# Attention and feed-forward on one core: the context halves and output turns of a step put in a new order, the last turn held into the next step, the output transposes halved

## Chip, cores, metric

One core of a Trainium2 chip. The metric is the device time of one execution in microseconds (us); lower is better. Ratios between kernels are the mean time of one kernel's fast runs over the mean of the other's fast runs of the same rounds, so they are not quite the ratio of the medians quoted beside them.

## The reference, cut to what matters

```python
xn = layernorm(x)                                   # x: 2048 x 640
# 32 heads of 192; keys and values are the last 512 rows of the caches
q = xn @ wq
p = softmax(q_h @ k_h.T * 192**-0.5)                # per head
s = concat_h(p @ v_h) @ wo                          # 6144 -> 640
g = silu((silu(xn @ w_gate) * (xn @ w_up)) @ w_down)
out = x + s * g
```

## The kernel before

After the feed-forward part (some 168 us) the kernel works through 16 pairs of heads (`pr`), and in each pair through 4 blocks of 512 query rows (`b`); a step is `i = 4 * pr + b`. A pair has two stages. First come the scores of its four steps, woven with the q blocks of the steps after. Then come the four context and output stages. A step's output uses the transposed context of two steps earlier.

Every matmul of these stages contracts 64 rows and runs beside a partner on the other half of the array ("row tiles"); only in the context and output stages of the last two pairs is the full array used. The two partners write different banks of PSUM, the matmul's accumulator memory. In contexts and outputs they change banks after the first "turn", so a second turn may start only when the first has ended. That is enforced by a tiny GpSimd memset which waits for the first turn and for which the second turn waits. Other PE work stands between the turns to hide it.

There are two kinds of PSUM accumulators with two buffers each: "sc" (scores, output tiles) and "mm" (q blocks, contexts).

```python
psum = ctx.enter_context(tc.tile_pool(name="psum", bufs=2, space=bass.MemoryType.PSUM))
def sc_tile(): return psum.tile([P, 2, 512], f32, name="sc", tag="sc")
def mm_tile(): return psum.tile([P, 2, 512], f32, name="mm", tag="mm")
...
def pv(i, q2):                      # contexts of half q2: four parts of 8 matmuls; 0,1 are turn 0, 2,3 turn 1
    ...                             # part 0: acc = mm_tile() (sc_tile() in one early case)
    #   after part 1: turned(m, st)    after part 3: divide(i, q2, acc, ...)
def divide(i, q2, acc, alone):      # VectorE reciprocal, four ScalarE scalings into O_b (bufs=2)
    ...
    if pr == last or i == 0:        # transpose by halves
        nc.sync.dma_start_transpose(out=OT_b[:, 6*q2 : 6*q2+6, :], in_=O_b[:, 2*q2 : 2*q2+2, :, :]...)
    elif pr < last and q2 == 1:     # both halves at once, after the second
        nc.sync.dma_start_transpose(out=OT_b[:, :, :], in_=O_b[:, :, :, :]...)
...
def turned(m, st):                  # the first turn's last matmul -> a memset on GpSimd
    st["turn"] = nc.gpsimd.memset(turn_t[:], 0.0)
    follows(st["turn"], m)          # `after` makes the second turn follow the memset
def wo_tile(i, qt):                 # one output tile: two turns of six matmuls
    def first():
        st["sc"] = sc_tile()
        wo_turn(st, i, qt, 0)
    def second():
        wo_turn(st, i, qt, 1)
        ...                         # VectorE: s_t = s_t + sc
    return [first, second]
...
def woven(x, y, z):                 # x: a context half, y and z: two output tiles
    for part in (y[0], *x[:2], y[1], z[0], *x[2:], z[1]):
        part()
...
for pr in range(NPAIR):
    for b in range(NB):
        i = pr * NB + b
        for kc in range(KC):
            if kc < 3 and i + 1 < NS:
                q_rows(i + 1, kc)   # ten matmuls into mm_tile(), then a VectorE sum into qT
            scores(i, kc)           # six matmuls into sc_tile(), then a ScalarE Exp
            ...
    for b in range(NB):
        i = pr * NB + b
        if i < 2:
            two(pv(i, 0), pv(i, 1))
        else:
            for q2 in range(2):
                if pr < last - 1:
                    woven(pv(i, q2), wo_tile(i - 2, 2 * q2), wo_tile(i - 2, 2 * q2 + 1))
                else:
                    ...             # the last two pairs: full-array matmuls, no turns
        ...                         # loads for later pairs, on the same sync queue as the transposes
```

The softmax here doesn't subtract the row's maximum and nothing guards it: scores larger than these inputs give would overflow.

## Time and profile before

| | before |
|---|---|
| time, median of the runs at hand | 938.76 us (938.25 to 939.03) |
| profiled span | 936.9 us |
| PE busy | 98% of it |
| one undisturbed pair of heads | 47.67 us |

The pair is read from the table of engines by stretches of time. Its columns are the stretch and its length, then busy time (and instructions) of each engine, the granted clock, the share of DMA and the rate moved.

```profile
core 0: us, PE busy (x) PEld busy (x) DVE busy (x) ACT busy (x) POOL busy (x), PEclk, DMA share, GB/s
234.55:282.22 47.67, 47.21 (x664) 33.90 (x664) 32.76 (x46) 26.80 (x49) 2.36 (x24) 1.00 0.42 80
```

PE is idle for only 0.46 us of this pair by its rows. In the page's list of DMA issues the transposes of the context stand like this (the last number is the median from issue to landing):

```profile
OT_b<-O_b SPq DMA_TRANSPOSE x67, 3.8
```

In this document DVE is VectorE, ACT is ScalarE, POOL is GpSimd and SPq is the sync engine's queue. Line 428 is the q block, 442 the scores, 446 the Exp, 468 the contexts. Line 568 (563 where the code is five lines shorter) is the output turn.

### The profile page before, as it was taken

Reading aid. Unit: us, or ns where it says so; the run is one execution under the profiler, and the core shown is the slowest. Engines: PE = TensorE matmul, PEld = TensorE weight load, DVE = VectorE, ACT = ScalarE, POOL = GpSimd, SP = SyncE. Lnnn points to the kernel's source line nnn. Section 1 sums busy time; section 2 is a strip of 40 time slices with the busy share of each in tenths; the row PEclk is TensorE's granted clock in tenths of the full one; section 3 lists DMA queues with packets and bytes.
Section 4 is the critical chain, followed back from the end, with each engine's and each line's share of the span. In section 5 each row is a group of like instructions: output and inputs, shape, how many; then the busy total and the mean of one; then the engine's idle time right before and its main releaser. Section 6 shows DMA issues by size and latency. Waiting matters only on the chain.

```text
span 936.9 us, 25618 instructions
## 1 busy us (share of the span) xinstructions
PE 920.3 (98%) x11101; PEld 613.0 (65%) x11101; DVE 576.7 (62%) x844; ACT 474.5 (51%) x847; POOL 100.2 (11%) x387
## 2 busy tenths in 40 slices
PE   9999999999999999999999999999999999999998
PEld 5455556474858575858686767576767767666665
DVE  6433321567676767676667666676767676767655
ACT  4222223646464646464646565555555555556561
POOL 0000000000100000000000000000000000002977
PEclk9999999999999999999999999999999999999999
DMA  9321510053534334443435253527161716163524
GB/s 296 69 60 27 113 34 1 1 101 63 92 71 88 75 73 90 72 92 66 97 59 105 55 109 50 113 35 129 36 127 32 129 25 135 25 128 91 133 57 138
DMA packets 241921, 77.17 MB, mean 82 GB/s; under 512 B 222736, under 2 KB 241808, under 8 KB 241808
## 3 DMA queue, kind: packets, MB, share of 16 engines
q1 hardware_dynamic: 240752, 74.71, 38.5%
q8 instruction: 87, 1.43, 0.6%
q10 hardware_dynamic: 1056, 0.82, 0.3%
q14 instruction: 26, 0.21, 0.1%
HBM read 39.45 MB, written 2.62 MB: 45 GB/s over the span
## 4 chain that ended last, share of the span: by engine, by line
PE 94%; DMA 3%; ACT 2%; DVE 1%; issue 0%; SPq 0%; DVEq 0%
PE mm L428 22%; PE sc L568 18%; PE sc L442 17%; PE mm L468 14%; PE sc L276 11%; PE mm L298 6%; PE sc L542 3%; DMA OT_b<-O_b 3%; PE mm L525 2%; ACT p_t L446 1%; PE sc L219 1%; PE mm L276 0%; PE mm L311 0%; PE sc L525 0%; ACT O_b L498 0%
## 5 line engine op out<-in xcount | busy, mean ns | idle before, releaser
L446 ACT ACTIVATE p_t<-sc 128x1024 bf16<-128x1024 f32 x254 | 253.1, 1023 | 117.5 <-PE sc L442 117.4
L433 DVE TENSOR_REDUCE qT<-mm 128x512 bf16<-128x1024 f32 x189 | 231.3, 1224 | 102.5 <-PE mm L428 100.0
L498 ACT ACTIVATE O_b<-mm,r 128x192 bf16<-128x192 f32 x486 | 165.1, 422 | 207.6 <-issue 107.1
L428 PE MATMUL mm<-xnT,wq_p 64*128 64x512 bf16 x1890 | 236.8, 376 | 0.0
L568 PE MATMUL sc<-wo_p,OT_b 64*128 64x320 bf16 x2592 | 217.5, 296 | 10.6 <-ACT p_t L446 6.0
L593 DVE TENSOR_TENSOR sacc<-sacc,sc 128x640 f32<-128x640 f32 x200 | 164.2, 821 | 89.7 <-PE sc L568 89.7
L442 PE MATMUL sc<-qT,khat 64*128 64x512 bf16 x1524 | 197.4, 376 | 0.0
L468 PE MATMUL mm<-V_p,p_t 64*128 64x193 bf16 x3520 | 185.7, 242 | 0.0
L468 PEld LDWEIGHTS <-p_t 64*128 64x128 bf16 x3584 | 161.4, 93 | 11.2
L428 PEld LDWEIGHTS <-wq_p 64*128 64x128 bf16 x1890 | 101.4, 94 | 100.4 <-issue 0.8
L568 PEld LDWEIGHTS <-OT_b 64*128 64x128 bf16 x2592 | 135.9, 94 | 39.0 <-issue 9.9
L442 PEld LDWEIGHTS <-khat 64*128 64x128 bf16 x1536 | 82.4, 94 | 83.3
L556 POOL MEMSET turn_t<- 128x1 f32 x328 | 32.2, 98 | 709.4 <-PE sc L568 544.4
L284 DVE TENSOR_TENSOR hT<-sc,sg 128x512 bf16<-128x512 f32 x46 | 31.7, 690 | 85.2 <-ACT sg L283 85.1
L283 ACT ACTIVATE sg<-sc 128x512 bf16<-128x512 f32 x46 | 27.3, 596 | 72.4 <-PE sc L276 72.4
L276 PE MATMUL sc<-xnT,wg_sb 128*128 128x512 bf16 (+1 forms) x260 | 59.2, 354 | 0.0
L276 PE MATMUL sc<-xnT,wu_sb 128*128 128x512 bf16 (+1 forms) x260 | 59.1, 354 | 0.0
L298 PE MATMUL mm<-wd_sb,hT 128*128 128x320 bf16 x384 | 56.6, 299 | 0.0
L487 DVE RECIPROCAL r<-mm 128x4 f32<-128x4 f32 x124 | 22.7, 183 | 48.9 <-PE mm L468 35.7
L298 PEld LDWEIGHTS <-hT 128*128 128x128 bf16 x384 | 37.6, 98 | 18.9
L276 PEld LDWEIGHTS <-wu_sb 128*128 128x128 bf16 x285 | 26.4, 98 | 26.9
L276 PEld LDWEIGHTS <-wg_sb 128*128 128x128 bf16 x285 | 26.4, 98 | 23.1 <-DMA wg_sb<-in_B_w_gate_dram 0.2
(67 smaller groups left out, 373.3 us busy)
## 6 DMA issues: line engine op xcount, KB each, us to landing
wo_p<-in_A_wo_dram SPq DMA_DIRECT2D x16, 480.0 KB, 4.3
K_p<-in_A_k_cache_dram SPq DMA_DIRECT2D x32, 192.0 KB, 3.8
V_p<-in_A_v_cache_dram SPq DMA_DIRECT2D x32, 192.0 KB, 3.1
wq_p<-in_A_wq_dram SPq DMA_DIRECT2D x64, 80.0 KB, 3.4
wq_p<-in_A_wq_dram SPq DMA_DIRECT2D x16, 160.0 KB, 3.5
x_r<-in_A_x_dram SPq DMA_DIRECT2D x16, 160.0 KB, 4.0
x_t<-in_A_x_dram SPq DMA_DIRECT2D x14, 160.0 KB, 3.6
wd_sb<-in_B_w_down_dram SPq DMA_DIRECT2D x1, 1920.0 KB, 12.4
```

The lines of the kernel that those rows point to most:

```text
L276: nc.tensor.matmul(out, w_sb[:, c, f * P : (f + 1) * P], xnT[:, c, qc], start=(c == 0), stop=(c == NC - 1),)
L284: nc.vector.tensor_tensor(hTs[b][:, f, :], u, sg[:], ALU.mult)
L298: nc.tensor.matmul(dn[:, 0:HD], hTs[b][:, f, ti * P : (ti + 1) * P], wd_sb[:, f, cols], start=(f == 0), stop=(f == NF - 1),)
L428: nc.tensor.matmul(q_ps[:, h, :], pairs[pr]["wq"][r, c, j * P : (j + 1) * P], xnT[r, c, b * 512 : (b + 1) * 512], start=(c == 0), stop=(c ...
L433: nc.vector.reduce_sum(qTs[i][:, j, :], q_ps[:, :, :].rearrange("p h n -> p n h"), axis=AX.X)
L442: nc.tensor.matmul(sc[:, h, :], khat[r, j, ks], qT[r, j, :], start=(j == 0), stop=(j == 2))
L446: nc.scalar.activation(p_t[:, :, :], sc[:, :, :], ACT.Exp, scale=scale)
L468: m = nc.tensor.matmul(acc[:, k, h * 256 : h * 256 + Dh + 1], Ps[i][kc][r, h, qt * P : (qt + 1) * P], V_p[r, kc, h, 0 : Dh + 1], start=(p ...
L498: nc.scalar.activation(O_b[:, qt, h, :], a_k[:, h, 0:Dh], ACT.Copy, scale=r[:, k, h, :])
L556: st["turn"] = nc.gpsimd.memset(turn_t[:], 0.0)
L568: m = nc.tensor.matmul(ps[:, n, 0:HD], OTs[i][r, 3 * qt + j, :], pairs[i // NB]["wo"][r, j, n * HD : (n + 1) * HD], start=(turn == 0 and j ...
L593: nc.vector.tensor_tensor(s_t, s_t, sc[:, :, 0:HD], ALU.add)
```

## The change

The intent: contexts first, so that PE has work at a pair's start while both "sc" buffers still hold scores; one step as a unit of two context halves and four output tiles, with more room between a half and its transpose's use; transposes by halves, so that each starts as soon as its half is done. The step's last turn has no work left to hide its memset, so it is held into the next step.

```diff
@@ divide
-        if pr == last or i == 0:
-            nc.sync.dma_start_transpose(
-                out=OT_b[:, 6 * q2 : 6 * q2 + 6, :],
-                in_=O_b[:, 2 * q2 : 2 * q2 + 2, :, :].rearrange("p t h d -> p (t h d)"),
-            )
-        elif pr < last and q2 == 1:
-            nc.sync.dma_start_transpose(
-                out=OT_b[:, :, :], in_=O_b[:, :, :, :].rearrange("p t h d -> p (t h d)")
-            )
+        nc.sync.dma_start_transpose(
+            out=OT_b[:, 6 * q2 : 6 * q2 + 6, :],
+            in_=O_b[:, 2 * q2 : 2 * q2 + 2, :, :].rearrange("p t h d -> p (t h d)"),
+        )
@@
-    def woven(x, y, z):
-        for part in (y[0], *x[:2], y[1], z[0], *x[2:], z[1]):
+    def drop():
+        while held:
+            held.pop()()
+
+    def woven(i):
+        (a, b), (w, x, y, z) = (pv(i, 0), pv(i, 1)), (wo_tile(i - 2, qt) for qt in range(4))
+        for part in (*a[:2], drop, w[0], *b[:2], w[1], x[0], *a[2:], x[1], y[0], *b[2:], y[1], z[0]):
             part()
+        held.append(z[1])
@@ the main loop
                     q_rows(i + 1, kc)
+                    drop()
                 scores(i, kc)
...
+            elif pr < last - 1:
+                woven(i)
```

More of the change, by code (lines that the diff above doesn't have):

```diff
@@ L652, in store @@
             nc.sync.dma_start(out=out2[t * P : (t + 1) * P, :], in_=ob[:])
+    held = []
     def two(x, y):
@@ L690 @@
                 two(pv(i, 0), pv(i, 1))
+            elif pr < last - 1:
+                woven(i)
             else:
                 for q2 in range(2):
-                    if pr < last - 1:
-                        woven(pv(i, q2), wo_tile(i - 2, 2 * q2), wo_tile(i - 2, 2 * q2 + 1))
-                    else:
-                        pv_full(i, q2)
-                        wo_full(i - 2, 2 * q2)
-                        wo_full(i - 2, 2 * q2 + 1)
+                    pv_full(i, q2)
+                    wo_full(i - 2, 2 * q2)
+                    wo_full(i - 2, 2 * q2 + 1)
             if b == 0 and pr + 2 < NPAIR:
```

## The prediction

> **What bounds the kernel now.** I read the busy table first, then the chain of work that ended last, then who waited for whom on the TensorE (PE), then the order of time around each kind of wait.
>
> ```profile
> PE 920.3 (98%) x11101; PEld 613.0 (65%) x11101; DVE 576.7 (62%) x844; ACT 474.5 (51%) x847; POOL 100.2 (11%) x387
> ...
> PE 94%; DMA 3%; ACT 2%; DVE 1%; issue 0%; SPq 0%; DVEq 0%
> ```
>
> PE is busy 98% of a 936.9 us span and 94% of the chain is PE work; the change leaves the number and shapes of its matmuls as they are. So it can only win time in which PE stands still. A matmul's row lasts longer than its turn (the chain gives six of the 320-column ones 0.41 us although one row lasts 0.296), so part of each stall hides under the last row. I therefore measure stalls from start to start: next start minus the last start's regular pace. By this measure the blocks run at a pace set by columns alone: ten q matmuls take 1.08 us, six score matmuls 0.65, sixteen context matmuls (two "parts") 0.67, six output matmuls (one "turn") 0.405. A change between kinds costs about 0.01 us, so changes of order are nearly free. What stands out are two kinds of stall:
>
> ```profile
> PE sc L568 <- ACT p_t L446: 6.0, 13, 0.5
> PE sc L568 <- DMA OT_b<-O_b: 3.6, 5, 1.2
> PE sc L568 <- DVE sacc L593: 0.9, 1, 0.9
> ```
>
> Line 568 is the output turn. Thirteen times, once for each head pair from the second to the fourteenth, it waits for an Exp (line 446); six times for a transpose by DMA (the one put down to DVE is at 342.79 us, where a transpose issued at 337.30 landed 5.45 later). First kind, in order of time:
>
> ```profile
> 424.33 1.48 PE L442 MATMUL sc<-qT,khat 64*128 64x512 bf16 x12
> 424.55 1.22 DVE L433 TENSOR_REDUCE qT<-mm 128x512 bf16<-128x1024 f32 x1
> 425.20 1.94 ACT L446 ACTIVATE p_t<-sc 128x1024 bf16<-128x1024 f32 x2 [0.70 <-PE sc L442]
> ...
> 426.27 0.58 PE L568 MATMUL sc<-wo_p,OT_b 64*128 64x320 bf16 x6 [0.46 <-ACT p_t L446]
> 426.68 0.85 PE L468 MATMUL mm<-V_p,p_t 64*128 64x193 bf16 x16
> ```
>
> Twelve score matmuls need 1.29, so PE was free at 425.62 and started at 426.27: 0.65 lost, not 0.46. The output turn needs an "sc" accumulator, and both hold scores until the first of the two Exps ends (425.20 + 1.02 = 426.22, plus 0.05). The context parts behind it need an "mm" accumulator, free long before. Second kind:
>
> ```profile
> 576.69 5.32 DMA OT_b<-O_b
> 582.01 0.05 issue
> 582.06 0.58 PE sc L568 x6
> ```
>
> Here PE was free at 581.15 and lost 0.91. The transpose of block b=0 of a pair is used two steps later; the time is just enough at 3.7 us to landing and not at 4.7 to 5.5. From starts: 1.39 at 197.93, then 0.82, 1.04, 0.91, 0.25, 0.37 and 1.00 at 204.67, 342.79, 582.06, 629.97, 636.27 and 822.14. Sum 5.8. The chain's 3% of DMA (28 us) is mostly transfer time that lay beside PE work.
>
> **What the Trainium skill says.** "Perfetto Trace Analysis", Identifying the Most-Contended Engine: matmul busy share is no measure of the distance to roofline, since matmuls are pipelined. The trace agrees: 0.65 us of stall shows as 0.46 of idle. The same page, Optimization Strategy: a consistent bubble can mean too few buffers in SBUF or PSUM. The thirteen equal 0.65 us bubbles are that. "TensorEngine Tiling", Gotcha 1: PSUM Pressure: row tiles may not use one PSUM bank at once and software must synchronize. This is why each second turn waits for a small GpSimd memset; it needs other PE work between two turns of one accumulator. "DMA: Bandwidth & Descriptors", the anatomy section, has a fixed cost of about 2.0 us per transfer (stated for the GpSimd path). From this trace: a half transpose lands in 2.75 us, a whole one in 3.7, so 2 x 2.75 - 3.7 = 1.8 is fixed; a half is therefore not twice as quick.
>
> **The change part by part.** Write a, b for the two context halves of a step (four parts each) and w, x, y, z for its four output tiles (two turns each). Before: w a w x a x | y b y z b z. After: a, held z, w, b, w x, a, x y, b, y z, with z's second turn held over, placed after the next step's first a, or at a pair's end after the first q block of the next pair.
>
> 1. Context first at the pair's start. It fills the 0.65 with 0.67 us of work: PE is free at 425.62, ends a's parts at 426.29, and the "sc" tile is free at 426.27. The second next need of "sc" (x, at 426.29 + 0.405 + 0.67 + 0.405 = 427.77) comes after the second Exp's end at 427.15. b needs the last q sum, over at 425.77. Gain 13 x 0.65 = 8.4 us.
>
> 2. Earlier and halved transposes. The first half now leaves after a, not after b; it is needed 9.3 us after a's matmuls end (before: 6.3 after b's). It needs about 1.93 (reciprocal and four scalings, from the trace) + 2.75, at worst + 4.5: at most 6.4. The second half is needed later still. So the six later stalls vanish, 4.4 us. At 197.93 the transpose was already halved and lands at 197.88 in either order; only 0.67 of other work is put in front of it. Gain 0.65, and 0.74 stays.
>
> 3. What it adds: the held turn at 14 pair starts.
>
> ```profile
> 402.32 1.26 PE L428 MATMUL mm<-xnT,wq_p 64*128 64x512 bf16 x10
> ...
> 403.40 0.83 PE L442 MATMUL sc<-qT,khat 64*128 64x512 bf16 x6
> ...
> 403.62 1.23 DVE L433 TENSOR_REDUCE qT<-mm 128x512 bf16<-128x1024 f32 x1 [0.26 <-PE mm L428]
> ...
> 405.13 0.83 PE L442 MATMUL sc<-qT,khat 64*128 64x512 bf16 x6
> ```
>
> From q's start T = 402.32: the sum of q ends at 404.85 on VectorE. The addition of z's result (0.82 us) stands behind it in program order, so it ends at 405.67 and frees z's "sc" tile at 405.72. The second score block takes that very tile. It started at 405.13; with z's turn in front, 405.13 + 0.405 = 405.54. So PE waits 0.18: 14 x 0.18 = 2.5 us lost.
>
> 4. Some 57 whole transposes become 114 halves: sync-queue time per pair rises by 4 x (2 x 1.21 - 1.45) = 3.9 us of a 47.67 us pair, in a queue that is not full. No PE time.
>
> Sum: 8.4 + 4.4 + 0.65 - 2.5 = 10.9 us. 938.66 - 10.9 = 927.7. An undisturbed pair goes from 47.67 to about 47.20.
>
> **The rivals.** (i) The "mm" accumulator becomes the wait. Before, a's tile had 3.8 us from its last matmul to its next use; now x y b y z = 0.81 + 0.67 + 0.81 = 2.29. The trace shows the need:
>
> ```profile
> 428.16 0.85 PE L468 MATMUL mm<-V_p,p_t 64*128 64x193 bf16 x16
> ...
> 429.12 0.18 DVE L487 RECIPROCAL r<-mm 128x4 f32<-128x4 f32 x1 [0.32 <-PE mm L468]
> 429.38 1.36 ACT L498 ACTIVATE O_b<-mm,r 128x192 bf16<-128x192 f32 x4 [2.25 <-issue]
> ```
>
> PE goes on at 428.83; the scalings end at 430.74, 1.91 later, plus 0.05. Slack 0.3. Two divides now come 1.48 apart and ScalarE needs 1.36, which just fits. If 0.1 were missing on each of two tiles in 54 steps, it would cost 11 us and leave nothing: about 938. In 105 divides of the trace that I timed, three stand beside a DMA stall and of the others only two end later than 2.0, at 2.20 and 2.26, so I give it one chance in ten, mostly in part. (ii) The DMA wait comes back: halves queue behind loads of K and wq in the sync queue (1.45 and 3.3 us of issue). Against it, nearly 3 us of slack even at the slowest landing; if half of the stalls stayed: 930. (iii) The held turn costs nothing, if the addition runs ahead of the sum of q: 925.2. The built program's VectorE order speaks against it: q's sum stands first. (iv) The stall at the pair's start only moves: the context parts wait too, or the next "sc" does. Against it, q's sums are over by 425.77. That would give 934 to 936.
>
> **Range and chances.** All stalls that the change could remove come to 8.4 + 5.8 = 14.2, so below 924.4 nothing is left to win, and 2% faster (under 919.9) would need a gain that I don't see: 0.03. The counted costs lie between 924.7 and 932.5, where I expect it 8 times in 10. Slower by 2% (over 957) would need about 0.35 us lost per step: 0.01. Within 2%: 0.96.
>
> **What would show it.** Right: no wait of line 568's successor for an Exp at pair starts; context matmuls directly after the last scores; hardly any wait of the output turn for a transpose except one of about 0.7 near 198 us; a new wait of the scores for VectorE's addition, some 14 times 0.2 (less of it as idle, as the last row hides part); pairs 47.2 us long. Wrong: context matmuls that wait for ScalarE (rival i); pairs that are still 47.6; output turns that wait for transposes in the middle of pairs; q blocks that wait for ScalarE at pair starts.

## The result and the profile after

The changed kernel takes 927.28 us (median of 4 runs, 926.91 to 927.71) against 938.76 for the kernel before (4 runs). The ratio is 0.9879, with a 95% interval of 0.9861 to 0.9896: 1.2% faster, so within 2%, and 0.4 us from the predicted 927.7.

The busy table and the chain of the kernel after:

```profile
PE 917.3 (99%) x11085; PEld 624.9 (68%) x11101; DVE 575.6 (62%) x844; ACT 473.8 (51%) x847; POOL 100.1 (11%) x387
...
PE 98%; DMA 1%; DVE 0%; issue 0%; ACT 0%; DVEq 0%
```

The work of PE is the same; ScalarE has fallen from 2% of the chain to 0% and DMA from 3% to 1% (the 16 missing matmuls are records that the trace lacks; start times show holes of just one matmul there). Who waited for whom on PE, output turns:

```profile
PE sc L563 <- DMA OT_b<-O_b: 0.5, 1, 0.5
```

One wait with idle time is left of the output turns' nineteen, the one at 198 us. The pair's start, in order of time:

```profile
420.13 1.46 PE L442 MATMUL sc<-qT,khat 64*128 64x512 bf16 x11
...
420.98 1.94 ACT L446 ACTIVATE p_t<-sc 128x1024 bf16<-128x1024 f32 x2 [0.70 <-PE sc L442]
421.41 0.85 PE L468 MATMUL mm<-V_p,p_t 64*128 64x193 bf16 x16
...
422.08 0.59 PE L563 MATMUL sc<-wo_p,OT_b 64*128 64x320 bf16 x6
```

The contexts follow the scores, and their 0.67 us ends at 422.08, just after the first Exp frees an "sc" buffer (420.98 + 1.02 + 0.05 = 422.05). The output turn follows without a wait. The new cost is at the next stage's start, where the held turn comes behind a q block:

```profile
398.68 0.59 PE L563 MATMUL sc<-wo_p,OT_b 64*128 64x320 bf16 x6
398.90 1.23 DVE L433 TENSOR_REDUCE qT<-mm 128x512 bf16<-128x1024 f32 x1 [0.67 <-PE mm L428]
...
399.74 1.26 PE L428 MATMUL mm<-xnT,wq_p 64*128 64x512 bf16 x10
...
400.04 0.81 DVE L588 TENSOR_TENSOR sacc<-sacc,sc 128x640 f32<-128x640 f32 x1
400.91 0.82 PE L442 MATMUL sc<-qT,khat 64*128 64x512 bf16 x6
```

The second q block is over at 399.74 + 1.08 = 400.82 and the scores start at 400.91, 0.05 after the addition's end at 400.85: 0.09 lost. A whole pair:

```profile
212.44:259.56 47.12, 47.12 (x667) 33.79 (x664) 32.65 (x45) 26.77 (x49) 2.35 (x24) 1.00 0.55 95
```

By start times, PE's stalls over the pairs come to this:

| stall | before, us | after, us |
|---|---|---|
| pair starts, for an Exp (13) | 8.3 | 0 |
| output turn at 198 us, for a transpose | 1.37 | 0.71 |
| later output turns, for a transpose | 6 waits, 4.4 | 1 wait, 0.12 |
| second score block of a pair, for VectorE (14) | 0 | 1.2 |
| sum | 14.1 | 2.1 |

That is 12.0 us less. The profiled spans differ by 11.5; about 0.3 of the rest is a longer wait for a weight load at the very start of the kernel after (0.53 against 0.20), which the change does not touch. The new margin on the "mm" buffers is seen here:

```profile
424.63 1.00 PE L563 MATMUL sc<-wo_p,OT_b 64*128 64x320 bf16 x12
...
425.19 2.78 ACT L498 ACTIVATE O_b<-mm,r 128x192 bf16<-128x192 f32 x8 [2.27 <-issue]
...
426.57 3.53 SPq L501 DMA_TRANSPOSE OT_b<-O_b  x2
...
426.93 0.85 PE L468 MATMUL mm<-V_p,p_t 64*128 64x193 bf16 x16
```

After a's last matmul PE goes on at 424.63. ScalarE does the divides of a and b back to back; a's is over when its transpose issues, at 426.57. The next step's contexts want that buffer at 426.93, so 0.31 is left after the 0.05 that a release takes.

### The profile page after: what moved, and what is told of

Its sections match the earlier page's. It is cut to its first block, busy times and chain, and to the rows that moved or that the text cites. A ratio compares the mean times of both kernels' runs of the same rounds, so it can differ in the third digit from the quotient of the medians.

```text
span 925.4 us, 25770 instructions
## 1 busy us (share of the span) xinstructions
PE 917.3 (99%) x11085; PEld 624.9 (68%) x11101; DVE 575.6 (62%) x844; ACT 473.8 (51%) x847; POOL 100.1 (11%) x387
## 4 chain that ended last, share of the span: by engine, by line
PE 98%; DMA 1%; DVE 0%; issue 0%; ACT 0%; DVEq 0%
PE mm L428 22%; PE sc L563 19%; PE sc L442 18%; PE mm L468 16%; PE sc L276 11%; PE mm L298 6%; PE sc L537 3%; PE mm L520 2%; DMA wg_sb<-in_B_w_gate_dram 1%; PE mm L276 0%; PE mm L311 0%; DMA OT_b<-O_b 0%; PE sc L520 0%; DMA x_t<-in_A_x_dram 0%; DVE s_f L638 0%
## 5 line engine op out<-in xcount | busy, mean ns | idle before, releaser
L428 PEld LDWEIGHTS <-wq_p 64*128 64x128 bf16 x1890 | 105.6, 94 | 96.0 <-issue 0.5
L563 PEld LDWEIGHTS <-OT_b 64*128 64x128 bf16 x2592 | 139.9, 94 | 22.7 <-DMA OT_b<-O_b 1.1
L442 PEld LDWEIGHTS <-khat 64*128 64x128 bf16 x1536 | 85.6, 94 | 79.2 <-issue 2.9
```

The source lines that it names most:

```text
L428: nc.tensor.matmul(q_ps[:, h, :], pairs[pr]["wq"][r, c, j * P : (j + 1) * P], xnT[r, c, b * 512 : (b + 1) * 512], start=(c == 0), stop=(c ...
L442: nc.tensor.matmul(sc[:, h, :], khat[r, j, ks], qT[r, j, :], start=(j == 0), stop=(j == 2))
L563: m = nc.tensor.matmul(ps[:, n, 0:HD], OTs[i][r, 3 * qt + j, :], pairs[i // NB]["wo"][r, j, n * HD : (n + 1) * HD], start=(turn == 0 and j ...
```

## The experiments

All outputs are right. Kernels of one group shared one chip and the runs of the kernel before.

**1. The order alone** (group 1): the changed kernel with whole transposes.

```diff
-        nc.sync.dma_start_transpose(out=OT_b[:, 6*q2 : 6*q2+6, :], ...)
+        if pr == last or i == 0: ...halves...
+        elif pr < last and q2 == 1: ...whole...
```

> The changed kernel with whole transposes, as before, so the new order alone. My theory: the order alone gives the transpose enough time. It leaves after b and is needed 7.8 us after b's matmuls end (6.3 before), and needs 1.93 of divide plus 3.7 to 5.5 to landing, at most 7.4. So 927 to 928 us, and at most 0.5 us more of stall in the first pair. Rival: it was the halving that took the transpose off the path. Then four or more of the six mid-pair stalls stay and the time is 930 to 932.

Measured: 928.31 us (before: 938.81). No mid-pair wait is left from the second pair on, so the theory holds there. But one stall of 1.97 us appears at 205.89, in the first pair, four times what I allowed. The sync queue and the chain show why:

```profile
197.86 1.23 SPq L101 DMA_DIRECT2D K_p<-in_A_k_cache_dram  x2
199.18 3.60 SPq L507 DMA_TRANSPOSE OT_b<-O_b  x1
```

```profile
199.18 6.66 DMA OT_b<-O_b
205.84 0.05 issue
205.89 0.58 PE sc L568 x6
```

The whole transpose was issued at 199.18, behind loads of K, took 3.60 us in the queue and 6.66 to landing, more than the worst 5.5 of the kernel before. It is a wait that the kernel before has too (0.80 at 204.67, where this transpose took 5.50). How late it lands differs from trace to trace: with halves the stall at this place is 0.12 in the kernel after and 0 in its repeat, but 0.56 and 0.68 in two other repeats of experiment 9. So the halving matters at most in the first pair once the order is new, and that it is worth the 1 us between 928.31 and 927.28 is not shown: the two were timed in different groups, and one of the four runs here took only 927.41.

**2. The halves alone** (group 1): the kernel before with the changed `divide`.

```diff
-        if pr == last or i == 0: ...halves...
-        elif pr < last and q2 == 1: ...whole...
+        nc.sync.dma_start_transpose(out=OT_b[:, 6*q2 : 6*q2+6, :], ...)
```

> The kernel before with halved transposes and nothing else. My theory: the first half leaves after a and has 9.3 us instead of 6.3, so the six later stalls (4.4 us) vanish, the 13 pair starts keep 0.65 each and 198 us keeps 1.37: 938.8 - 4.4 = 934.4. Rival: the halves' extra issues and fixed costs lengthen the sync queue so that transposes come late again, or the order was what removed the stalls: 937 to 939.

Measured: 934.76 us, ratio to before 0.9958 (0.9944 to 0.9972).

```profile
PE sc L563 <- ACT p_t L446: 6.0, 13, 0.5
...
PE sc L563 <- DMA OT_b<-O_b: 1.2, 1, 1.2
```

The thirteen Exp waits stand as before, and of the seven transpose waits only the one at 198 us is left. With experiment 1 it follows that for the mid-pair waits the order and the halving are each enough alone; they don't add.

**3. The first output tile in another pool** (group 1): the kernel before, where the first output tile of 13 pairs takes an "mm" buffer.

```diff
-            st["sc"] = sc_tile()
+            st["sc"] = mm_tile() if qt == 0 and b == 2 else sc_tile()
```

> The kernel before, with the first output tile of each pair from the second to the fourteenth put into an mm accumulator instead of an sc one; order and transposes as before. My theory: the 0.65 us at pair starts is only the lack of an sc accumulator until the Exp ends, so 13 x 0.65 = 8.4 us go: 930.3, with the DMA stalls as before. Rival: PE waits there for something else too (the last q sum frees the other mm buffer at 425.8, or a drain between scores and outputs): 934 to 939.

Measured: 930.71 us, ratio 0.9914 (0.9900 to 0.9927).

```profile
421.68 1.46 PE L442 MATMUL sc<-qT,khat 64*128 64x512 bf16 x12
422.98 0.57 PE L568 MATMUL mm<-wo_p,OT_b 64*128 64x320 bf16 x6
```

The output turn starts 1.30 after the scores, their own pace. One changed line takes the 0.65 us out of all thirteen pair starts, so the bubble was only the lack of an "sc" buffer. The new order is one way to fill it, not the only one.

**4. The addition first** (group 1): the changed kernel with the held turn between q's matmuls and q's sum.

```diff
-    def q_rows(i, j):
+    def q_rows(i, j, between=None):
...                                  # the ten matmuls
+        if between:
+            between()
...                                  # the sum
-                    q_rows(i + 1, kc)
-                    drop()
+                    q_rows(i + 1, kc, drop)
```

> The changed kernel with the held turn put between q's matmuls and q's sum in program order, so that VectorE does z's addition before q's sum. My theory: the 14 new stalls of 0.09 us come from the addition standing behind the sum; they vanish and q's later sum has room: 927.3 - 1.3 = 926.0. Rival: the 0.09 is a cost of changing between q, output and score matmuls: no change, 927.3.

Measured: 926.52 us against 927.28 for the changed kernel in another group. That distance was too small for different chips, so it was run again (experiment 9). In the trace the cause is plain:

```profile
446.08 0.82 DVE L590 TENSOR_TENSOR sacc<-sacc,sc 128x640 f32<-128x640 f32 x1 [1.07 <-PE sc L565]
...
446.81 2.35 DVE L435 TENSOR_REDUCE qT<-mm 128x512 bf16<-128x1024 f32 x2
447.60 0.81 PE L444 MATMUL sc<-qT,khat 64*128 64x512 bf16 x6
```

The addition ends at 446.90, before the scores need the buffer at 447.60. All 14 stalls of 0.09 are gone.

**5. Both single edits on the kernel before** (group 2): experiments 2 and 3 together.

> The kernel before with both single edits: the first output tile of a pair in an mm accumulator, and halved transposes; the order of parts stays as it was. My theory: the two gains are of different stalls and add up, as measured 8.1 + 4.0: 938.8 - 12.1 = 926.7, about the time of the changed kernel, without any new order. Rival: the two overlap or a shifted transpose runs into a new wait: 928 to 931.

Measured: 926.82 us (before: 939.14), ratio 0.9868. Their gains add up. The old order, with two small edits, is as fast as the new one (0.9879), as far as these runs can tell them apart.

**6. No hold** (group 3): z's second turn at once.

```diff
-        held.append(z[1])
+        z[1]()
```

> The changed kernel without the hold: z's second turn follows directly on its first, at the end of each step. Theory: the second turn waits for GpSimd's memset. From the trace a turn's first start to the memset's start is 0.71 us, the memset takes 0.10, and 0.05 to go on: 0.86, where six matmuls need 0.405, so 0.45 lost per step, 54 steps: 24.5, less the 1.3 of the pair starts: 927.3 + 23.2 = 950. Rival: the wait is hidden by PE's weight loads or by the order, and the hold is worth little: 927 to 932.

Measured: 950.55 us (before: 939.24), slower than either kernel.

```profile
PE sc L563 <- POOL turn_t L551: 15.3, 54, 0.3
```

All 54 steps wait for the memset, 0.45 us each by start times, 24.1 in all. Without the hold the new order would have lost 1.2%, so it gains nothing unless the last turn is held.

**7. More work for ScalarE in the changed kernel** (group 3), to measure the margin on the "mm" buffers.

```diff
             for h in range(2):
-                nc.scalar.activation(O_b[:, qt, h, :], ...)
+                for _ in range(2 if k else 1):
+                    nc.scalar.activation(O_b[:, qt, h, :], ...)
```

> The changed kernel with each of the last two scalings of a divide done twice (the same result written again), so ScalarE needs six instead of four per divide, about 0.63 us more. Theory: the new order left the mm accumulators 0.3 us of slack, so each step from the second of a pair on now stalls by some 0.3 to 0.8 us, 54 steps: 943 to 970. Rival: the slack is larger than I say, or ScalarE is not what frees the tile: 927 to 930.

Measured: 983.80 us, more than I allowed.

```profile
PE mm L468 <- ACT O_b L499: 33.7, 80, 0.7
PE mm L428 <- ACT O_b L499: 4.7, 14, 0.3
```

By start times these 94 stalls hold 55.3 us. They are of two kinds, as one step shows:

```profile
444.02 4.42 ACT L499 ACTIVATE O_b<-mm,r 128x192 bf16<-128x192 f32 x12 [2.22 <-DVE r L487]
446.34 0.84 PE L468 MATMUL mm<-V_p,p_t 64*128 64x193 bf16 x16 [0.34 <-ACT O_b L499]
448.49 0.74 PE L468 MATMUL mm<-V_p,p_t 64*128 64x193 bf16 x13 [0.50 <-ACT O_b L499]
```

Six scalings take 2.26 us where four took 1.36, so the two cost 0.90 and not my 0.63. A wait for a's buffer holds 0.52 in most cases (54 waits, the 14 of the q blocks among them). By 0.90 - 0.52 the margin there was 0.38, near the 0.31 read above. A wait for b's buffer holds 0.67 (40 of them) and says nothing of the margin: b's divide stands directly behind a's on ScalarE and takes 4.42 - 2.26 = 2.16, where the two halves come 1.48 apart. So a step pays twice, some 1.2 us in all; that, with the price of a scaling, is what I missed.

**8. The same in the kernel before** (group 3).

> The kernel before with the same doubled scalings. Theory: there the tile had 3.8 us for 1.96 and the doubled scalings fit in it, but the transposes leave 0.63 us later, with the time for them just enough before: the two waits per pair (blocks b=0 and b=1) return at about 0.5 us in most pairs, 26 waits: 938.8 + 8 to 16 = 947 to 955. Rival: nothing but the accumulators counts, and the time stays at 939.

Measured: 957.97 us, 3 above the range I gave.

```profile
PE sc L569 <- DMA OT_b<-O_b: 8.4, 10, 2.1
PE mm L428 <- ACT O_b L499: 7.3, 14, 0.9
```

The transposes come late more often, as expected: 19 waits between output turns hold 9.9 us by start times, where six held 4.4. I had missed the second line. At a pair's end b's buffer is wanted by the second q block after one turn, a q block and a score block, 0.405 + 1.08 + 0.65 = 2.13 us, not 3.8; with 1.96 + 0.90 needed, 0.73 is missing by this sum. The trace has 14 waits there, most of 0.67, 9.6 us in all. So the same extra ScalarE work costs the kernel before 18.7 us and the changed one 56.5: the change spent margin. Whether the kernel of experiment 5, as fast and in the old order, keeps the old margin was not run.

**9. Three on one chip** (groups 2 and 4). A mixed version: the new order in the first pair alone, where it halves the stall at 198 us; from then on the old order with the first output tile in an "mm" buffer; halves and the addition first.

```diff
-            elif pr < last - 1:
+            elif pr == 0:
                 woven(i)
+            elif pr < last - 1:
+                for q2 in range(2):
+                    woven_before(pv(i, q2), wo_tile(i - 2, 2 * q2), wo_tile(i - 2, 2 * q2 + 1))
```

> A version made to beat both: the new order in the first pair alone, where it halves the stall at 198 us (1.37 to 0.7), with the held turn's addition ahead of q's sum, and from the second pair on the old order with the first output tile in an mm accumulator; halved transposes throughout. Theory: nothing is left but the 0.7 at 198 us and the waits of the last pair, as in the version with the addition first (926.5 by median): 926.0, give or take 0.5. If the wait for the mm accumulator of the old order returns, 927 or more.

Measured (group 2): 926.20 us, ratio 0.9864. Then the changed kernel, the addition first and the mixed version on one chip:

> The changed kernel once more, on one chip with the two versions below, because their distances of about 1 us are smaller than what runs of different calls can tell apart: 927.3 give or take 0.5.

> The changed kernel with the held turn's addition ahead of q's sum, again: 1.2 us under the changed kernel of this call if the 14 stalls of 0.09 that left the trace are all that differs; 0 if they were given back elsewhere.

> The mixed version again: its trace keeps the same stalls as the one with the addition first, so the same time within 0.5 us, and about 1.2 us under the changed kernel.

Measured: 926.97 us (926.64 to 927.52), 925.95 (925.63 to 926.68) and 926.31 (926.00 to 926.54), with 938.83 before. The addition first is 1.0 us under the changed kernel by medians, near the 1.2 that its 14 stalls held. Four runs each, with ranges that just touch, make this likely but not certain: the intervals of the ratios (0.9874, 0.9862, 0.9866, each about 0.0016 to either side) overlap. The two improved versions can't be told apart. Both are 1.3 to 1.4% faster than the kernel before.

## Why the prediction was right

It was right in time and, mostly, in its terms. That the total came within 0.4 us is in part luck: the errors below have opposite signs.

- *Only stalls can be won.* The stalls by start times fell by 12.0 us, the spans by 11.5. The counted floor (924.4) held for every version that ran. A change between kinds of matmul costs no more than the 0.01 us it allowed; most show 0.00 by start times.
- *Step 1, contexts first:* predicted 8.4, found 8.3. Experiment 3 shows the cause by another remedy: the buffer, not the Exp as such.
- *Step 2, transposes:* predicted 4.4 + 0.65, found 4.3 + 0.66. What was left unsaid is which half of the change does it. Experiments 1 and 2 show that either does from the second pair on. In the first pair the landing varies too much between traces to say. The "worst" landings were no bounds: the step allowed 4.5 us for a half, and those needed two steps later took up to 4.79 in the trace after, without a stall. The expectation of experiment 1 allowed 5.5 for a whole one, and one took 6.66.
- *Step 3, the held turn:* the mechanism was right (experiment 4 removes it), the size was not: 0.09 each instead of 0.18, so 1.2 us instead of 2.5. The step let the addition start at the end of the sum's row. In the trace it starts at 400.04, where that row ends at 398.90 + 1.23 = 400.13. The Trainium skill puts the end of a VectorE row at the write's acknowledgement ("Perfetto Trace Analysis", Per-engine timelines); the trace agrees that the next row does not wait for it, by 0.09 us here. This error is worth 1.3 us. Against it stand 0.3 us of the start's weight load and about 0.5 of small remainders.
- *Step 4, more transposes:* no PE wait appeared; each lands in 2.8 us by median instead of 3.8.
- *Rival (i)*, the "mm" buffer: it did not come true, and its margin of 0.3 reads 0.31 in the trace after and 0.38 by experiment 7. *Rival (ii)*, late transposes behind loads, came true in the first pair alone: 0.12 us in the trace after, 0.56 and 0.68 in two repeats of experiment 9 with halves, 1.97 in experiment 1 without. *Rival (iii)* is refuted by the 14 waits of the trace after, *rival (iv)* by its pair starts.

## What to carry to other kernels

When PE is 98% busy, list its stalls by start times and price each by itself: that list is the ceiling of what a new order can bring, and it shows which single edit (a buffer from another pool, an earlier transfer) would win the same. A new order that fills one wait can take time from another buffer's release; work out that margin, because here it fell to 0.3 us and two extra scalings per divide on ScalarE cost three times as much as before. Put the instruction that frees a scarce buffer ahead of one that nobody awaits yet.

## What the Trainium skill lacked or had wrong

- "Perfetto Trace Analysis", Identifying the Most-Contended Engine, says that matmul busy time is no measure of the distance to roofline, but not how to find the stalls that it hides. Here a stall showed as 0.46 us of idle and was 0.65 by start times, and one of 0.09 showed as none.
- "TensorEngine Tiling", Gotcha 1: PSUM Pressure, says that software must keep row tiles from using one PSUM bank at once, and gives no price. Through a GpSimd memset it costs here 0.45 us for each pair of turns of six 320-column matmuls when no other PE work stands between them (54 times in experiment 6).
- "DMA: Bandwidth & Descriptors", the anatomy section, gives the fixed cost of about 2.0 us for the GpSimd path. No page has a measured time to landing for transposes like these from the sync queue: in the kernel before half ones landed in 2.75 us and whole ones in 3.7, so 1.8 is fixed by this estimate, but a single one behind loads took 6.66 (experiment 1).
